# A token-mixing kernel on Trainium2: the entry of the three rounds of chunks is spread differently over the steps

## The chip, the cores and the metric

The kernel runs on one core of a Trainium2 chip. Its time is the device time of one execution in microseconds (us); several runs give a median. The engines are named as in the profile: PE (TensorE, matrix products), DVE (VectorE), ACT (ScalarE), POOL (GpSimd) and SP (SyncE, which here only issues transfers). Transfers between the HBM and the on-chip buffers run on 16 DMA engines; SP, POOL and ACT each have a queue into them and issue in order.

## The reference

First a short causal convolution along the sequence with softmax weights for each of 8 heads, then a phase-aware mixing of tokens and channels. B = 8, S = 4224, D = 192:

```python
out = np.einsum('hk,bskhg->bshg', w, x_unf)         # 7 taps for each of 8 heads
theta = x @ w_theta                                 # x is that result
zr, zi = x * np.cos(theta), x * np.sin(theta)
y = np.einsum('ts,bsd->btd', w_tok_r, zr) + np.einsum('ts,bsd->btd', w_tok_i, zi)
u = x + y
return u + np.maximum(u @ w_ch, 0.0)
```

Nearly all the work is in the two products with 4224 x 4224 matrices, over 8 x 192 = 1536 columns.

## The kernel before

**Tiles.** The sequence is cut into 33 *chunks* of 128 tokens for the inner (source) side and into 33 row blocks of 128 tokens for the output side. A chunk takes 4 pieces of 32 tokens from 4 places of the sequence, so that the weight matrix can be turned in 32 x 32 blocks on DVE. Of each chunk seven half-width tiles are kept in on-chip memory (`z`, one *slot* of 11): the raw products of x with cosine and sine, and sums of them. The two matrices are applied two row blocks (a *unit*) at a time by a scheme with seven multiplications in place of eight, as in Strassen's, whose weight sums (`S1` to `S4`, `wsum`) and z sums (`T1` to `T4`, `sums`) are made on DVE.

**Rounds and steps.** Only 11 chunks are held at a time, so the work goes in three *rounds* of 11 chunks, each of which has to meet all 17 units (16 pairs and one single row block). A *step* t handles one unit `u = (t + shift) % 17` with all chunks that are active at that step: chunk k is active from `start[k]` for 17 steps. `start` comes from the list `base`: chunks enter one or two at a step. In a round's change the old chunks leave and the new ones enter a little later, and n, the number of active chunks, is below 11. There are 58 steps. A step of a pair goes through seven *runs* (`runs`) of n *products* each; a product is two matmuls of 384 columns (L536). At the end of each run of a pair a bank of PSUM is *given* (`give`): DVE adds 128 x 768 values to the sums in `pv` (L461). In the first round some gives are copies on ACT. Three names c1, c2, c3 share two PSUM buffers:

```python
("11", Z11, "c1", True, (0, 0, True)),   ("S1", T1, "c2", True, (1, 1, True)),
("S2", T2, "c1", False, (0, 1, True)),   ("S4", Z22, "c2", False, (0, 1, False)),
("S3", T3, "c1", False, (1, 1, False)),  ("12", Z21, "c3", True, (0, 0, False)),
("22", T4, "c1", False, (1, 0, True)),
```

So c1 is added to in run 7 after the give of run 5 has read it, and c3 in run 6 needs the buffer of c2, which the give of run 4 reads.

**What lies around the products.** The steps' products are one stream (`stream`, `mix`); other work is put into it by hand. `step_events(t)` gives each task a place in sevenths of the step, and the task is emitted before the first product past that place. PE, DVE and ACT keep the order of emission (`in_order`); transfers on SP and chunk loads on POOL may be moved by the scheduler. For a step these are:
- the weights: `load_w` of step t + 2 on POOL (4 DMAs for each matrix; the buffer `st` is free when the turn of the step before has read it), and the turns (L387) and sums (L399) of step t + 1 on DVE (`w_tasks`);
- the sums: `load_rows` brings `pv` of step t + 1 from HBM (`part`), and at a step's end `pv` is stored there; in the last 17 steps it goes on to the output instead. `pv` and the chunks' x tiles `xw` share six buffers (tag `big`);
- the adding of x to the sums: `load_x` and `add_x` (POOL), or for late steps `add_ahead`, two accumulating DMAs on POOL for a row block;
- the chunks: x is loaded (`load_chunk`, 4 DMAs on POOL, and 4 copies on SP of the 16 tokens before each piece out of the chunk before), then built by `tasks`: two convolutions on PE (L216) and their evacuation on ACT, a transpose (L170, ACT), for each half of the columns a theta product on PE (L146) and two sines on ACT (L291), two products with x on DVE (L297), four sums on DVE (L306). `places` gives their places in the step before the chunk enters; with two chunks in a step there are two rows of places.

**The first round** is built ahead of the stream, in a loop over chunks (L812 to L861): between the build's tasks, `between(n)` emits up to n products of the steps whose chunks are ready, 11 at most in one turn of the loop. The `pv` tiles of steps 0 and 1 lie in slots of `z` that later chunks take.

Of the kernel before, what the change touches and what calls it, by code (L numbers as in the profile page):

```python
# [11 lines left out]
F16 = mybir.dt.float16  # L12
# [4 lines left out]
def kernel(  # L17
# [44 lines left out]
    PC = 512  # L62
    NP = 4

    base = [0, 0, 1, 1, 2, 3, 3, 4, 4, 5, 5]
    assert len(base) == NW
    start = [base[k % NW] + (NU + 1) * (k // NW) for k in range(NK)]
    NSTEP = start[-1] + NU
    shift = (NU - 1 - (NSTEP - 1)) % NU

# [109 lines left out]
    Z11, T1, Z21, Z22, T2, T4, T3 = range(7)  # L180
    Z12 = T3

    class Chunk:


# [22 lines left out]
        def conv(self, j):  # L208

            if j == 0:  # L210
                self.z = zpool.tile([P, 7, HN], F16, name="z", tag="z")
                self.x = self.z[:, T2 : T2 + 2, :].rearrange("p t n -> p (t n)")
            pc = banks("pc")
            for h in range(4):
                for half in range(2):
                    pe(nc.tensor.matmul(  # L216
                        pc[half * 2 * Q : (half + 1) * 2 * Q, h // 2,
                           h % 2 * B * G : (h % 2 + 1) * B * G],
                        lhsT=bands[:, 4 * j + h, :, :].rearrange("p a m -> p (a m)"),
                        rhs=self.xw[:, half, :, (4 * j + h) * G : (4 * j + h + 1) * G],  # L220
                        start=True, stop=True,
                    ))
            evacuate(
                self.x.rearrange("p (b d) -> p b d", d=D)[
                    :, :, 4 * j * G : 4 * (j + 1) * G
                ].rearrange("p b (i h g) -> p i h b g", i=2, h=2),
                pc[:, :, 0 : 2 * B * G].rearrange("p i (h b g) -> p i h b g", h=2, b=B),
                self.k == 1 or (self.k in (2, 3) and j == 1),
            )
            if j == 1:  # L230
                self.store()

        def conv_batches(self, g):

            if g == 0:
                self.z = zpool.tile([P, 7, HN], F16, name="z", tag="z")
# [97 lines left out]
    class Step:  # L334


        def __init__(self, t):
# [185 lines left out]
        def mix(self, events):  # L523
# [120 lines left out]
    def step_events(t):  # L644
# [15 lines left out]
        if t in (NPS, NPS + 1):  # L660
            for j, k in enumerate(k for k in range(NK) if start[k] <= NPS):
                for o, a, b, at in (
# [4 lines left out]
                        (1.3 + 1.4 * j if t == NPS else 1.2 + 0.6 * j) + at,  # L667
                        lambda k=k, o=o, a=a, b=b: chunks[k].sum(o, a, b),
                    ))
        if t == NU - 2:  # L670
            def load_wch():
                dve(nc.vector.memset(wch[:, 1:3, :], 0.0))
# [5 lines left out]
            if 0 <= begin < steps[t].time:  # L678
                found.append((7 * begin / steps[t].time, f))
        if t >= NU - 2:  # L680
            new = [k for k in range(NK) if start[k] == t + 2 and k >= NW]
            for k in new:
                found.append((4.5, lambda k=k: load_chunk(k)))
            places = (
                (.1, .1, 1.1, 2.75, 3.05, 3.6, 3.65, 3.9, 4.1),
                (2.1, 2.1, 3.55, 4.6, 5.0, 5.5, 5.55, 5.8, 6.0),
            )
            new = [k for k in range(NK) if start[k] == t + 1 and k >= NW]
            for k, pos in zip(new, places):

                def add(at, j, k):
# [16 lines left out]
    noise = zpool.tile([P, BH], F16, name="noise", tag="z")  # L708
# [76 lines left out]
    flow = stream()  # L785
    need = [None]

    def more(n):

        for i in range(n):  # L790
            if need[0] is None:
                need[0] = next(flow, NK)
            if need[0] > ready[0]:
                return n - i
            need[0] = next(flow, NK)
        return 0

    steps[0].load_rows()
# [4 lines left out]
    for m in (1, 2):  # L803
        steps[1].load_w(m)
    load_chunk(4)
    load_chunk(5)
    for g in range(NG):
        chunks[0].conv_batches(g)
    idle(2)
# [2 lines left out]
    for i in range(1, NW + 2):  # L812
        ch = chunks.get(i) if i < NW else None
        old = chunks[i - 1] if i <= NW else None

        def between(n):
            left = more(n)
            if i < 3:
                idle(min(left, 2) if i == 1 else 0)

        if ch:
            ch.conv(0)
        between(2)
# [6 lines left out]
        between(2)  # L830
# [7 lines left out]
        between(1)  # L838
        if i == 1:
            for first in (Z11, Z21):  # L840
                old.product(first, slice(0, 1))
# [4 lines left out]
                old.product(first, slice(1, 2))  # L846
        elif old:
            old.product(Z11)
        between(2)
# [5 lines left out]
        between(1)  # L855
        if old and start[i - 1] > NPS:
            old.sums(0)
        between(1)
        if old and start[i - 1] > NPS:
            old.sums(1)  # L860
        between(1)  # L861
    ready[0] = NK
    for _ in flow:
        pass
# [31 lines left out]
```

## Time and profile before

| | |
|---|---|
| median of 3 runs | 1435.88 us (1433.75 to 1436.91) |
| the profiled execution | 1437.8 us, span 1436.0 us, mean granted clock 0.999 |
| PE busy | 1409.4 us, 98% |
| DVE busy | 973.0 us, 68% |
| ACT, POOL busy | 310.6 us and 434.3 us |
| DMA | 281.99 MB, 196 GB/s on the mean |

The profile is one execution taken by the hardware profiler. Instructions are grouped by line, engine, operation and tile, with the number, the busy time, the mean of one and the idle time before them with what ended it. A busy PE is not PE at its peak, since matmuls are pipelined and their ends are modelled. The DMA share is the mean busy share of the 16 engines; it can pass 1 where packets of several queues overlap.

### The profile page before, as it was taken

Reading aid. Unit: us, or ns where it says so; the run is one execution under the profiler, and the core shown is the slowest. Engines: PE = TensorE matmul, PEld = TensorE weight load, DVE = VectorE, ACT = ScalarE, POOL = GpSimd, SP = SyncE. Lnnn points to the kernel's source line nnn. Section 1 sums busy time; section 2 is a strip of 40 time slices with the busy share of each in tenths; the row PEclk is TensorE's granted clock in tenths of the full one; section 3 lists DMA queues with packets and bytes.
Section 4 is the critical chain, followed back from the end, with each engine's and each line's share of the span. In section 5 each row is a group of like instructions: output and inputs, shape, how many; then the busy total and the mean of one; then the engine's idle time right before and its main releaser. Section 6 shows DMA issues by size and latency. Waiting matters only on the chain.

```text
span 1436.0 us, 23771 instructions
## 1 busy us (share of the span) xinstructions
PE 1409.4 (98%) x9829; PEld 889.7 (62%) x9829; DVE 973.0 (68%) x1046; ACT 310.6 (22%) x374; POOL 434.3 (30%) x655
## 2 busy tenths in 40 slices
PE   8889999999999999999999999999999999999997
PEld 5556666666666666666666666666566666666665
DVE  6893554545548787866665657877777677767676
ACT  5851101111124244000000004335100110010133
POOL 8511211111233332532333343233323123213110
PEclk9999999999999999999999999999999999999999
DMA  9975766564799999898899889999999999999894
GB/s 193 234 164 132 147 125 128 100 151 89 147 232 227 231 236 239 209 256 177 232 236 229 229 157 243 231 198 255 248 206 216 215 206 220 203 202 197 166 214 136
DMA packets 272045, 281.99 MB, mean 196 GB/s; under 512 B 106688, under 2 KB 240192, under 8 KB 271936
## 3 DMA queue, kind: packets, MB, share of 16 engines
q0 software_dynamic: 162464, 92.15, 48.8%
q1 hardware_dynamic: 71840, 178.88, 35.4%
q10 hardware_dynamic: 37632, 9.44, 4.5%
q8 instruction: 77, 1.26, 0.4%
q14 instruction: 32, 0.26, 0.1%
HBM read 245.49 MB, written 108.13 MB: 246 GB/s over the span
## 4 chain that ended last, share of the span: by engine, by line
PE 92%; DMA 2%; DVE 2%; ACT 1%; SPq 1%; issue 1%; POOL 0%; DVEq 0%; ACTq 0%; POOLq 0%
PE y L536 84%; PE v L146 5%; PE tp L170 1%; PE pc L216 1%; ACT z L291 1%; DMA xw<-in_x_dram 1%; DMA xw<-xw 1%; SPq L194 1%; DVE pv L461 0%; DVE z L306 0%; DVE pv L585 0%; DMA part<-pv 0%; DMA st<-in_moe_w_tok_r_dram 0%; DMA wsb<-in_weight_dram 0%; DVE wt L399 0%
## 5 line engine op out<-in xcount | busy, mean ns | idle before, releaser
L536 PE MATMUL y<-z,wt 128*128 128x384 f16 x7672 | 1282.4, 326 | 6.4 <-DVE pv L461 5.3
L536 PEld LDWEIGHTS <-wt 128*128 128x128 f16 x7672 | 743.7, 98 | 482.6 <-issue 6.3
L461 DVE TENSOR_TENSOR pv<-y,pv 128x768 f32<-128x768 f32 x317 | 302.5, 954 | 323.9 <-PE y L536 284.0
L387 DVE STREAM_TRANSPOSE wt<-st 128x1408 f16<-128x1408 f16 (+7 forms) x224 | 327.5, 1465 | 51.0 <-PE y L536 38.3
L374 POOL DMA_DIRECT2D st<-in_moe_w_tok_r_dram x232 | 132.3, 578 | 463.5 <-DVE wt L387 451.8
L374 POOL DMA_DIRECT2D st<-in_moe_w_tok_i_dram x232 | 132.4, 579 | 405.0 <-DVE wt L387 396.5
L399 DVE TENSOR_TENSOR wt<-wt 128x1408 f16<-128x1408 f16 (+6 forms) x208 | 173.4, 834 | 40.5 <-PE y L536 38.3
L156 ACT ACTIVATE z<-pc 128x768 f16<-128x768 f32 (+1 forms) x62 | 47.5, 803 | 387.0 <-PE pc L216 378.4
L156 ACT ACTIVATE ub<-pv 128x768 f16<-128x768 f32 x63 | 50.2, 836 | 343.6 <-DVE pv L461 315.9
L459 ACT ACTIVATE pv<-y 128x768 f32<-128x768 f32 x66 | 53.7, 814 | 280.5 <-PE y L536 280.5
L146 PEld LDWEIGHTS <-uT 128*128 128x128 f16 x1056 | 90.6, 98 | 23.8 <-issue 5.9
L439 POOL TENSOR_TENSOR pv<-pv,xr 128x1536 f32<-128x1536 f32 x24 | 74.5, 3103 | 66.2 <-issue 26.7
L203 POOL DMA_DIRECT2D xw<-in_x_dram x132 | 76.3, 587 | 27.1 <-issue 7.0
L585 DVE SCALAR_TENSOR_TENSOR pv<-v,pv 128x768 f32<-128x768 f32 (+1 forms) x67 | 62.8, 942 | 24.9 <-PE v L146 24.5
L306 DVE TENSOR_TENSOR z<-z 128x768 f16<-128x768 f16 x132 | 71.2, 552 | 2.2
L291 ACT ACTIVATE z<-v,half_pi 128x768 f16<-128x768 f32 x66 | 59.6, 903 | 56.4 <-PE v L146 55.7
L156 ACT ACTIVATE uT<-tp 128x1536 f16<-128x1536 f16 (+1 forms) x47 | 56.5, 1208 | 47.3 <-PE tp L170 47.3
L297 DVE TENSOR_TENSOR z<-z 128x1536 f16<-128x1536 f16 (+1 forms) x68 | 60.6, 926 | 4.3 <-ACT z L291 4.2
L146 PE MATMUL v<-wth,uT 128*128 128x192 f16 x528 | 54.4, 246 | 2.7 <-ACT z L291 2.1
L146 PE MATMUL v<-wch,uT 128*128 128x192 f16 x528 | 54.3, 246 | 1.3 <-DVE pv L585 0.7
L291 ACT ACTIVATE z<-v 128x768 f16<-128x768 f32 x66 | 53.2, 806 | 0.0
L216 PE MATMUL pc<-xw,bands 96*64 96x192 f16 x512 | 30.4, 251 | 5.4 <-DMA st<-in_moe_w_tok_r_dram 2.7
(45 smaller groups left out, 144.8 us busy)
## 6 DMA issues: line engine op xcount, KB each, us to landing
part<-pv SPq DMA_DIRECT2D x79, 768.0 KB, 4.3
pv<-part SPq DMA_DIRECT2D x79, 768.0 KB, 6.0
out_dram<-pv SPq DMA_DIRECT2D x65, 384.0 KB, 4.5
st<-in_moe_w_tok_r_dram POOLq DMA_DIRECT2D x136, 176.0 KB, 6.0
st<-in_moe_w_tok_i_dram POOLq DMA_DIRECT2D x136, 176.0 KB, 5.3
xs<-z SPq DMA_DIRECT2D x132, 96.0 KB, 5.1
xw<-in_x_dram POOLq DMA_DIRECT2D x121, 96.0 KB, 6.2
xr<-xs SPq DMA_DIRECT2D x24, 384.0 KB, 4.5
```

The costliest lines, as they stand in the source:

```text
L146: pe(nc.tensor.matmul(v[:, k, b * D : (b + 1) * D], lhsT=tT[:, 3 * k + b + i, :], rhs=w[:, 2 * b + i, :], start=(i == 0), stop=(i == 1),))
L156: act(nc.scalar.activation(out=out, in_=in_, func=AT.Copy))
L203: nc.gpsimd.dma_start(out=self.xw[lo : lo + n, h, :, :], in_=x[:, t0 : t0 + n, :].rearrange("b s d -> s b d"),)
L291: act(nc.scalar.activation(**args))
L306: dve(nc.vector.tensor_tensor(out=z[:, o, :], in0=z[:, a, :], in1=z[:, b, :], op=ALU.subtract))
L374: pool(nc.gpsimd.dma_start(out=st[a * Q : (a + 1) * Q, 0:nb, :, 0:n] .rearrange("i r bt s -> i (r bt) s"), in_=w[self.tbs[0] * P : (self.t ...
L387: dve(nc.vector.transpose(self.w[name][:, 0 : self.n, :, :], self.st[int(name[1])][:, int(name[0]) - 1, :, 0 : self.n * Q] .rearrange("p b ...
L399: dve(nc.vector.tensor_tensor(out=self.w[name][:, 0 : self.n, :, :], in0=self.w[a][:, 0 : self.n, :, :], in1=self.w[b][:, 0 : self.n, :, : ...
L439: ins = pool(nc.gpsimd.tensor_tensor(out=self.pv[i], in0=self.pv[i], in1=self.xr[i], op=ALU.add))
L461: dve(nc.vector.tensor_tensor(out=o, in0=yv, in1=o, op=ALU.add))
L536: pe(nc.tensor.matmul(y[cn][:, q, 0:BH], lhsT=self.w[wn][:, c, :, :].rearrange("p bt i -> p (bt i)"), rhs=chunks[k].z[:, zn, q * BH : (q + ...
L585: dve(nc.vector.scalar_tensor_tensor(out=ub[:, ks, :], in0=v[:, ks, :], scalar=0.0, in1=ub[:, ks, :], op0=ALU.max, op1=ALU.add,))
```

## The change

There are now three lists of entries. In the first and second round one chunk enters at a step (after the first four, which enter in pairs), over eight steps instead of five; in the third round entries run from step 39 to 44. The number of steps becomes 61. A new list `build` says in which step a chunk is built: in the first two rounds, as before, the step ahead of its entry; in the third round from step 35 on, mostly one chunk a step, up to four steps ahead of the entry. Chunk loads go into the step ahead of the build as before, but at 1.25 sevenths of it instead of 4.5.

In the loop of the first round `between(n, upto)` no longer emits a fixed number: `reach` counts the products that chunks up to a given one allow, and the products that the newest usable chunk has opened are spread over the whole turn of the loop. Chunk loads in the loop come one turn later.

The `z` slots are taken once ahead of all work (`slots`), and `pv` of steps 0 and 1 and the noise tile lie in named slots. The stores of the sums of steps 0 and 1 (`keep`) are emitted in steps 3 to 6. The window in which x is added early (`quiet`) begins four steps sooner relative to the second round's last entry, and the last nine steps instead of five have x added ahead by accumulating DMAs, one step's row blocks in each of steps 27 and on, the others in step 44.

```diff
-    base = [0, 0, 1, 1, 2, 3, 3, 4, 4, 5, 5]
-    assert len(base) == NW
-    start = [base[k % NW] + (NU + 1) * (k // NW) for k in range(NK)]
+    bases = ([0, 0, 1, 1, 2, 3, 4, 5, 6, 7, 8],
+             [0, 0, 1, 1, 2, 3, 4, 5, 6, 7, 8],
+             [3, 3, 4, 4, 5, 6, 6, 7, 7, 8, 8])
+    start = [b + (NU + 1) * r for r, base in enumerate(bases) for b in base]
+    build = [s - 1 for s in start]
+    build[2 * NW :] = [
+        2 * (NU + 1) + b for b in (-1, -1, 0, 1, 2, 3, 4, 5, 6, 6, 7)
+    ]
...
+    slots = [ztile() for _ in range(NW)]
...
-                self.z = zpool.tile([P, 7, HN], F16, name="z", tag="z")
+                self.z = slots[self.k] if self.k < NW else ztile()
...
-            quiet = [v for v in visits if start[2 * NW - 1] < v <= 2 * NU]
+            quiet = [v for v in visits if start[2 * NW - 1] - 4 < v <= 2 * NU]
+            ahead = t >= NSTEP - 9
...
-                if not self.late:
+                if not ahead:
                     self.adds.append(i)
                 else:
                     far = known <= start[2 * NW - 1]
-                    self.ahead.append((i, 2 * NU - NW + 2 * (t % NU) if far else start[-1],
+                    self.ahead.append((i, start[2 * NW - 1] + t - NSTEP + 10 if far else start[-1],
...
-                    pv = zpool.tile([P, N], F32, name="pv", tag="z")
+                    z = slots[NW - 1 - 2 * self.t - len(self.pv)]
+                    pv = z.rearrange("p t n -> p (t n)")[:, 0 : 2 * N].bitcast(F32)
...
-            if not self.final:
-                for i, tb in enumerate(self.tbs):
-                    nc.sync.dma_start(
-                        out=part[(self.t // NU) % 2][tb, :, :], in_=self.pv[i]
-                    )
+            if not self.final and self.t > 1:
+                for i in range(len(self.tbs)):
+                    self.keep(i)
+
+        def keep(self, i):
+            nc.sync.dma_start(
+                out=part[(self.t // NU) % 2][self.tbs[i], :, :], in_=self.pv[i]
+            )
...
+        if 2 < t < 7:
+            found.append((1, lambda: steps[(6 - t) // 2].keep((6 - t) % 2)))
...
-            new = [k for k in range(NK) if start[k] == t + 2 and k >= NW]
-            for k in new:
-                found.append((4.5, lambda k=k: load_chunk(k)))
+            for k in range(NW, NK):
+                if build[k] == t + 1:
+                    found.append((1.25, lambda k=k: load_chunk(k)))
...
-            new = [k for k in range(NK) if start[k] == t + 1 and k >= NW]
+            new = [k for k in range(NW, NK) if build[k] == t]
...
+    def reach(r):
+
+        return next((i for i, k in enumerate(chunk_of) if k > r), len(chunk_of))
...
-        def between(n):
-            left = more(n)
-            if i < 3:
-                idle(min(left, 2) if i == 1 else 0)
+        lo, hi = reach(i - 3), reach(i - 2)
+
+        def between(n, upto):
+            left = more(max(0, round(lo + (hi - lo) * upto / 13) - done[0]))
+            if i == 1:
+                idle(min(n, 2))
...
-        between(2)
+        between(2, 0)
...
-        if i + 3 < NW:
-            load_chunk(i + 3)
-        between(1)
+        if i > 2:
+            load_chunk(min(i + 2, NW - 1))
+        between(1, 4.5)
...
```

More of the change, by code (lines that the diff above doesn't have):

```diff
@@ L63 @@
     NP = 4
-    base = [0, 0, 1, 1, 2, 3, 3, 4, 4, 5, 5]
-    assert len(base) == NW
-    start = [base[k % NW] + (NU + 1) * (k // NW) for k in range(NK)]
+    bases = ([0, 0, 1, 1, 2, 3, 4, 5, 6, 7, 8],
[6 more added lines that the diff above has]
+    ]
+    assert len(start) == NK and all(
+        start[k] + NU <= build[k + NW] < start[k + NW] for k in range(NK - NW)
+    )
     NSTEP = start[-1] + NU
@@ L181, with ztile @@
     Z12 = T3
+    def ztile():
+        return zpool.tile([P, 7, HN], F16, name="z", tag="z")
+    slots = [ztile() for _ in range(NW)]
     class Chunk:
@@ L235, in conv_batches @@
             if g == 0:
-                self.z = zpool.tile([P, 7, HN], F16, name="z", tag="z")
+                self.z = slots[self.k] if self.k < NW else ztile()
                 self.x = self.z[:, T2 : T2 + 2, :].rearrange("p t n -> p (t n)")
@@ L546, in mix @@
                 f()
-            if not self.final:
-                for i, tb in enumerate(self.tbs):
-                    nc.sync.dma_start(
-                        out=part[(self.t // NU) % 2][tb, :, :], in_=self.pv[i]
-                    )
+            if not self.final and self.t > 1:
[4 more added lines that the diff above has]
+                out=part[(self.t // NU) % 2][self.tbs[i], :, :], in_=self.pv[i]
+            )
         def cast_half(self, i, h, gs, by_dve):
@@ L707 @@
         nc.sync.dma_start(out=stage[i // 2][rows, i % 2, :], in_=part_w)
-    noise = zpool.tile([P, BH], F16, name="noise", tag="z")
+    noise = slots[NW - 5][:, 0, 0:BH]
     nc.vector.memset(noise, 0.0)
@@ L786 @@
     need = [None]
+    done = [0]
+    chunk_of = [s.ks[item[3]] for s in steps for item in s.products()]
+    def reach(r):
+        return next((i for i, k in enumerate(chunk_of) if k > r), len(chunk_of))
     def more(n):
@@ L795, in more @@
             need[0] = next(flow, NK)
+            done[0] += 1
         return 0
@@ L805 @@
     load_chunk(4)
-    load_chunk(5)
     for g in range(NG):
@@ L826 @@
         ready[0] = i - 2
-        between(1)
+        between(1, 1)
         if ch:
             ch.conv(1)
-        between(2)
+        between(2, 3)
         if old:
@@ L835 @@
                 steps[i // 2].turn(name)
-        if i + 3 < NW:
-            load_chunk(i + 3)
-        between(1)
+        if i > 2:
+            load_chunk(min(i + 2, NW - 1))
+        between(1, 4.5)
         if i == 1:
@@ L848 @@
             old.product(Z11)
-        between(2)
+        between(2, 6.5)
         if i > 1 and old:
@@ L854 @@
                 steps[i // 2].turn(name)
-        between(1)
+        between(1, 8)
         if old and start[i - 1] > NPS:
             old.sums(0)
-        between(1)
+        between(1, 9.5)
         if old and start[i - 1] > NPS:
             old.sums(1)
-        between(1)
+        between(1, 11)
     ready[0] = NK
```

## The prediction, written before the result was known

> **What bounds the kernel now.** I read the busy times first, then a table of stretches, then the waits of TensorE, then one step instruction by instruction.
>
> ```profile
> PE 1409.4 (98%) x9829; PEld 889.7 (62%) x9829; DVE 973.0 (68%) x1046; ACT 310.6 (22%) x374; POOL 434.3 (30%) x655
> L461 DVE TENSOR_TENSOR pv<-y,pv 128x768 f32<-128x768 f32 x317 | 302.5, 954 | 323.9 <-PE y L536 284.0
> ```
> TensorE (PE) is busy for 98%, so only the few places where it is not are worth anything. The stretches (columns: busy us of PE, weight load, DVE, ACT, POOL; clock; DMA share; GB/s) find them:
> ```profile
> 20.90:105.20 84.30, 74.13 (x662) 48.39 (x661) 71.73 (x105) 62.77 (x78) 36.51 (x64) 1.00 1.07 207
> 105.20:410.00 304.80, 304.80 (x1878) 183.54 (x1876) 153.32 (x135) 40.51 (x50) 66.08 (x116) 1.00 0.65 133
> 415.30:572.00 156.70, 156.70 (x1255) 103.31 (x1254) 121.16 (x148) 68.58 (x78) 47.63 (x84) 1.00 1.00 233
> 861.60:992.40 130.80, 130.80 (x1042) 86.01 (x1040) 101.27 (x123) 55.46 (x63) 43.19 (x76) 1.00 1.00 224
> 992.40:1038.40 46.00, 42.97 (x316) 27.10 (x314) 35.98 (x39) 13.57 (x16) 16.01 (x24) 1.00 1.04 267
> 1060.00:1340.00 280.00, 280.00 (x1887) 179.33 (x1886) 198.38 (x193) 31.53 (x40) 76.87 (x91) 1.00 0.97 207
> ```
> PE never idles in either change of rounds up to 992 us, nor in the long stretches: nothing can be gained there, only lost. Idle are the entry of the first round (20.9 to 105.2) and 3.0 us in steps 40 and 41. Counting the L536 pairs against the steps' sizes, a product (two matmuls) takes 0.325 us. A chunk's build takes PE 0.79 (convolutions) + 0.67 (transposes) + 2 x 0.66 (thetas) + some 0.17 at the seams = 2.95 us. The entry holds 132 products, 42.9 us, and 398 other matmuls, 9.05 chunks at 44 each, 26.7 us: 69.6 of 84.3, so **14.7 us are lost there**, most of it inside "busy".
>
> The waits of PE name what it falls behind when it idles:
> ```profile
> PE y L536 <- DVE pv L461: 5.3, 5, 1.9
> PE pc L216 <- DMA st<-in_moe_w_tok_r_dram: 2.7, 2, 2.3
> PE pc L216 <- DMA xw<-xw: 2.7, 2, 2.0
> ```
> And this is how close DVE stands in step 39 (966.2 to 992.4; nine active chunks, two being built). First ACT's sines of the first chunk, then DVE, then PE:
> ```profile
> 977.64 0.90 ACT L291 ACTIVATE z<-v,half_pi 128x768 f16<-128x768 f32 x1 [1.53 <-PE v L146]
> 978.44 0.80 ACT L291 ACTIVATE z<-v 128x768 f16<-128x768 f32 x1
> 979.28 0.90 ACT L291 ACTIVATE z<-v,half_pi 128x768 f16<-128x768 f32 x1
> ```
> ```profile
> 980.21 1.83 DVE L297 TENSOR_TENSOR z<-z 128x1536 f16<-128x1536 f16 x2 [0.96 <-ACT z L291]
> 982.55 0.96 DVE L461 TENSOR_TENSOR pv<-y,pv 128x768 f32<-128x768 f32 x1 [0.51 <-PE y L536]
> 983.42 2.20 DVE L306 TENSOR_TENSOR z<-z 128x768 f16<-128x768 f16 x4
> 985.54 1.37 DVE L387 STREAM_TRANSPOSE wt<-st 128x1152 f16<-128x1152 f16 x1
> 986.84 0.92 DVE L461 TENSOR_TENSOR pv<-y,pv 128x768 f32<-128x768 f32 x1
> ```
> ```profile
> 976.78 0.82 PE L146 MATMUL v<-wth,uT 128*128 128x192 f16 x8
> 986.59 6.01 PE L536 MATMUL y<-z,wt 128*128 128x384 f16 x36
> ```
> Run 7 adds to the bank that the fifth give (986.84 to 987.76) reads. Run 6 began at 986.59 and has nine products, so run 7 begins at 989.52: the fifth give was ready 1.8 us before it was needed. That chain (theta, sines, two products, give, four sums, turn, give) is fixed in length; PE's way to run 7 shrinks with the number n of active chunks. The change makes n small exactly while third-round chunks are built.
>
> **The change, part by part.** Work on PE is equal (19660 instruction rows in both programs, the same tables of products); steps go from 58 to 61. The sum is against the profiled execution, 1437.8 us (span 1436.0, 1.8 around it), which lies 1.9 over the median of the three runs, 1435.88.
>
> *Third round: built at steps 35 to 43, entered at 39 to 44.* Between, n is 9, 7, 6, 5, 6, 7, 7, 8, 9 in steps 35 to 43 (before: 9 or 10 in 35 to 40). The order of DVE in the built program is that shown above in each of them. In a step with one build, the first theta follows item 14, 17 or 20 for n = 5, 6, 7; so it starts at n=5 14 x 0.325 + 0.79 + 0.67 + 0.17 = 6.2 us after the step begins, at n=6 7.15, at n=7 8.1. From it to the end of the third sine are 3.40 us (976.78 to 980.18), and then 0.03 + products 1.74 + give 0.87 + sums 2.12 + turn + give 0.92. The turn is for the next step's n', less 0.07 of overlap; these rows exist:
> ```profile
> L387 DVE STREAM_TRANSPOSE wt<-st 128x896 f16<-128x896 f16 x8 | 8.8, 1102 | 0.0
> L387 DVE STREAM_TRANSPOSE wt<-st 128x768 f16<-128x768 f16 x4 | 3.9, 969 | 0.0
> L387 DVE STREAM_TRANSPOSE wt<-st 128x640 f16<-128x640 f16 x4 | 3.4, 842 | 7.0 <-DMA st<-in_moe_w_tok_r_dram 5.0 <-PE y L536 2.1
> ```
> Run 7 could begin at 6n x 0.325 + 2.95 us. Step 38 (n=5, n'=6): give ready at 6.2 + 3.4 + 5.65 + 0.9 = 16.15, run 7 at 12.7: 3.45 lost. Step 37 (6, 5): 17.0 against 14.65, 2.35. Step 39 (6, 7): 2.65. Step 36 (7, 6): 18.1 against 16.6, 1.5. Step 40 (7, 7): 1.65. Step 41 (7, 8; its turn between the rows of 896 and 1152 columns, 1.2): 1.8. **Sum +13.4 us**. The same sum for n=10 with one build leaves 1.2 us to spare, so the second round's entry (n=10, steps 19 to 25) costs 0; if a row is half a microsecond worse it still costs nothing, and it cannot gain. Ends for the third: 0, if all of it were hidden as in 861 to 992, and +25, if transfers come late too (below). I take +13.4, since every term is a row of the neighbouring step.
>
> *Steps 43 and 44 for 40 and 41.* One build instead of two stands in the short step: DVE has 1.83 + 2.2 us less, PE 2.95 less. Before, 3.0 us idle there, partly a turn that waited 3.1 us for its weights. The last give of the short step's first bank comes some 2 us late now, and weights may again: 2 to 5 us, against 3.0. I take no difference, ends -2 and +3.
>
> *First round, a chunk a step, products spread over each build.* In the slot after chunk 1's convolution there is nothing, then 4, 20, 4, 24, 36, 43, 50, 57, 64, 71 products (before: 4, then 9 and 11 each). From the sixth on PE has 14.6 us or more of its own in each build, and ACT (two evacuations, four sines, one turn: 1.51 + 3.40 + 1.45 = 6.4, and gives at 0.81) no longer sets the pace. What stays lost: slots of four products, PE 4.25 against ACT 6.4, about 1.2 in the one and 2.2 in the other; chunk 5's load, which now stands on POOL behind the weights of step 2 (issued at 30.8 to 33.2 before), so it is issued by 35.5, lands in 6.2 (median of xw loads) at 41.7, where it is wanted at about 41: 1 to 2; DVE, which in slots 5 and 6 has about 10.6 and 14.9 us of turns, sums, products and gives against PE's 10.7 and 14.6 and starts 3 behind, because it waits for step 2's weights as it did before (5.0 us): 3. With 1 for later slots that is 9 of the 14.7: **-5.7 us**. Ends: -12, if only the slots of four stay, and +2, if the longer ramp waits for weights at each step.
>
> *First sums stored late.* The four stores of steps 0 and 1 (768 KB, 6.8 us to land in this stretch) are written later in the program, but in the built order of SP one still stands ahead of chunk 5's copies of history, one behind them. They free no buffer that PE waits for; their row blocks are read 17 steps later. Before, two stores held up SP to 31.5 and 38.7 us, and chunk 5's convolution idled 2.0 for xw<-xw. This is inside the -5.7; alone its ends are -2 and +1.
>
> *Chunk loads a step ahead.* On POOL they now stand between a step's two weight loads, 4 issues of 0.58 = 2.3 us ahead of the second, which waits for the turn at 4.2 sevenths of its step anyway. In 861 to 992 they landed in 8.0 us at the median with no PE idle. 0, ends 0 and +3 (if the second load comes those 2.3 late).
>
> *Additions and traffic.* Adds of x on POOL go from 24 to 19 (3.1 each, never on the path), adding DMAs from 18 to 28, 14 of them in step 44 where 8 stood in step 41. PE had no idle from 1024 on with eight in flight; 0, ends 0 and +4. Six more stores and six more loads of sums lie in full steps or in the narrow ones.
>
> Total +13.4 - 5.7 = +7.7: 1445.5 as that execution counts, **1444 us as a median**.
>
> **The rivals.** *The entry wins (faster).* If DVE's chain were covered, the entry alone would decide: 3 in the middle and -9 at the front give 1430. For it: DVE was 101.3 of 130.8 us busy in 861 to 992, and with one build a step instead of two its load per build interval falls. Against it: the chain is of latencies in one step, not of load. It decides once steps 36 to 41 lose under 5.7 together. The Trainium skill's page Perfetto Trace Analysis, section Optimization Strategy, says that where the most contended engine changes over time, interleaving the regimes may help; by that rule spreading both entries gains, and the time is this rival's. In the entry the rows agree with it, in steps 36 to 41 I think not.
>
> *The DMA engines bind in the narrow steps (slower still).* Each step moves four 768 KB blocks whatever its n, 128 packets of 6 KB at 234 ns each: 7.5 us of 16 engines; weights for n=7 are 2048 packets at 55 ns, 7.0 us; chunk load, history and store 5. That is 19.5 us in step 38, against 17.8 with DVE's loss. For it: share 1.00 already in 861 to 992. Against: 20.9 to 105.2 ran at 1.07. It would add 2 to 3 us in four steps: 1453. The packet records show 704 bytes in 74 ns, 448 in 55, 320 in 46: smooth. The Trainium skill's DMA: Bandwidth & Descriptors, section Specifications, puts line rate at 512 bytes and more, with read-modify-write below; at twice the price for n of 7 and less the steps would need some 26 us, an estimate that gives about 1480. The records do not bear that out.
>
> *The entry gains nothing.* The ramp waits for weights instead: 1449. For it: two waits for st in the list above.
>
> **How the numbers follow.** The forecast 0.60 (1439 to 1449 by its terms), entry wins 0.18, DMA binds 0.12 (0.02 of it for 1480), no gain in the entry 0.10. About 0.2% (2.9 us) is what a measurement here can tell from no change. Faster by more takes most of the second case, 0.16; within it 0.07, from the edges of the first two; slower 0.77. The range 1431 to 1454 reaches from the faster case's time to just past the DMA case.
>
> **What would show it.** Right: steps 36 to 41 last 17 to 18 us with PE waiting for the give (L461's successor) just before run 7, most in step 38; PE loses 8 to 10 us rather than 14.7 up to the first step that runs at full rate. Wrong: no PE wait for DVE near 770 to 890 us, or waits there that end with a transfer; an entry that loses 15 again, with PE waiting for xw or DVE for st.

## The result and the profile after

The changed kernel takes **1461.39 us** (1460.85 to 1461.98 in four runs), the kernel before 1435.87 beside it: a ratio of 1.018, with a 95% interval of 1.0162 to 1.0197. Slower was right, but 25.5 us instead of the 8 forecast, and the time lies above the range of 1431 to 1454. The profiled execution of after has a span of 1459.1 us, 23.1 more than that of before; the other 2.4 are no part of the two traces, since the profiled execution of before lay 1.9 over its median and that of after 0.5 under.

The first fence shows lines of the page of after, the second its table of stretches (columns as before: busy us of PE, weight load, DVE, ACT and POOL; clock; DMA share; GB/s), the third the waits of PE over the whole span.

```profile
PE 1412.2 (97%) x9829; PEld 889.9 (61%) x9829; DVE 995.9 (68%) x1091; ACT 310.5 (21%) x374; POOL 442.7 (30%) x684
L476 DVE TENSOR_TENSOR pv<-y,pv 128x768 f32<-128x768 f32 x338 | 322.2, 953 | 315.7 <-PE y L551 275.1
```
```profile
20.80:100.00 79.20, 72.04 (x599) 45.86 (x597) 59.75 (x87) 50.95 (x64) 38.83 (x68) 1.00 1.16 222
534.00:593.00 59.00, 55.02 (x391) 34.45 (x389) 46.74 (x47) 13.17 (x16) 23.21 (x26) 1.00 0.92 220
850.00:1070.00 220.00, 200.06 (x1491) 127.64 (x1490) 172.43 (x212) 67.26 (x78) 76.38 (x128) 1.00 1.06 252
1080.00:1360.00 280.00, 280.00 (x1887) 179.34 (x1886) 199.41 (x194) 31.53 (x40) 69.90 (x91) 1.00 0.94 201
```
```profile
PE y L551 <- DVE pv L476: 23.1, 19, 2.1
PE v L154 <- DMA uT<-ub: 6.8, 1, 6.8
```

PE's busy time is nearly the same; what grew is its idle time: in the second round's entry (534 to 593 us), where it had none before, in the third round's (850 to 1070), where it had 3.0 us, and in one long wait for a transfer after that. A step begins with its first L551 product, so each step's length can be read from the trace and compared with its products at 0.325 us and 2.95 us for each chunk built. (Steps with a build that lose nothing come out 0.07 us short for each chunk, so a build really takes 2.88; differences that small count as nothing below.) For before and after this gives (us):

| where | before | after | difference |
|---|---|---|---|
| first round, time up to the first step at full rate (4 before, 8 after) less the products ahead of it | 62.3 | 58.3 | -4.1 |
| steps 22 and 23 (10 chunks, one built) | none lost | 27.91 and 27.78 long, their neighbours 25.63 | +4.4 |
| step 28 | 0 | 0.7 | +0.7 |
| third round, steps 36 to 41 | 0 (36, 37, 39) | 1.34, 2.18, 3.94, 3.49, 2.84, 1.76 | +15.55 |
| last steps of that entry (38, 40, 41 before; 43, 44 after) | 3.7 | 1.7 | -2.1 |
| step 45 | as its neighbours | 36.22 long, its neighbours 27.66 | +8.6 |

The sum is +23.1, the difference of the spans. Two of the rows, +4.4 and +8.6, are not in the prediction at all.

### The profile page after: what moved, and what is told of

The parts are those of the page before. It is cut to its first block, busy times and chain, and to the rows that moved or that the text cites. A ratio compares the mean times of both kernels' runs of the same rounds, so it can differ in the third digit from the quotient of the medians.

```text
span 1459.1 us, 23864 instructions
## 1 busy us (share of the span) xinstructions
PE 1412.2 (97%) x9829; PEld 889.9 (61%) x9829; DVE 995.9 (68%) x1091; ACT 310.5 (21%) x374; POOL 442.7 (30%) x684
## 4 chain that ended last, share of the span: by engine, by line
PE 81%; DMA 8%; DVE 7%; issue 1%; POOL 1%; ACT 1%; SPq 0%; DVEq 0%; POOLq 0%; ACTq 0%
PE y L551 73%; PE v L154 5%; DVE pv L476 2%; DVE wt L401 2%; DVE z L310 1%; PE tp L178 1%; DMA uT<-ub 1%; PE pc L229 1%; DVE z L319 1%; DMA xs<-z 1%; DMA xw<-xw 1%; DMA st<-in_moe_w_tok_i_dram 1%; DMA part<-pv 1%; DMA xr<-xs 1%; DVE wt L413 1%
## 5 line engine op out<-in xcount | busy, mean ns | idle before, releaser
L551 PE MATMUL y<-z,wt 128*128 128x384 f16 x7672 | 1285.9, 326 | 25.8 <-DVE pv L476 23.1
L551 PEld LDWEIGHTS <-wt 128*128 128x128 f16 x7672 | 743.5, 98 | 506.4 <-issue 24.9
L476 DVE TENSOR_TENSOR pv<-y,pv 128x768 f32<-128x768 f32 x338 | 322.2, 953 | 315.7 <-PE y L551 275.1
L401 DVE STREAM_TRANSPOSE wt<-st 128x1408 f16<-128x1408 f16 (+8 forms) x236 | 328.8, 1398 | 43.2 <-PE y L551 35.9
L388 POOL DMA_DIRECT2D st<-in_moe_w_tok_i_dram x244 | 139.6, 580 | 449.5 <-DVE wt L401 428.8
L388 POOL DMA_DIRECT2D st<-in_moe_w_tok_r_dram x244 | 139.5, 579 | 420.9 <-DVE wt L401 410.3
L413 DVE TENSOR_TENSOR wt<-wt 128x1408 f16<-128x1408 f16 (+7 forms) x220 | 173.0, 786 | 47.2 <-PE y L551 45.0
L474 ACT ACTIVATE pv<-y 128x768 f32<-128x768 f32 x58 | 47.1, 812 | 211.1 <-PE y L551 210.4
L454 POOL TENSOR_TENSOR pv<-pv,xr 128x1536 f32<-128x1536 f32 x19 | 59.9, 3152 | 58.5 <-DVE pv L603 16.4
L319 DVE TENSOR_TENSOR z<-z 128x768 f16<-128x768 f16 x132 | 74.4, 574 | 2.2
L310 DVE TENSOR_TENSOR z<-z 128x1536 f16<-128x1536 f16 (+1 forms) x68 | 63.6, 967 | 5.1 <-ACT z L304 5.0
```

The source lines that it names most:

```text
L310: dve(nc.vector.tensor_tensor(out=o, in0=xv, in1=o, op=ALU.mult))
L319: dve(nc.vector.tensor_tensor(out=z[:, o, :], in0=z[:, a, :], in1=z[:, b, :], op=ALU.subtract))
L388: pool(nc.gpsimd.dma_start(out=st[a * Q : (a + 1) * Q, 0:nb, :, 0:n] .rearrange("i r bt s -> i (r bt) s"), in_=w[self.tbs[0] * P : (self.t ...
L401: dve(nc.vector.transpose(self.w[name][:, 0 : self.n, :, :], self.st[int(name[1])][:, int(name[0]) - 1, :, 0 : self.n * Q] .rearrange("p b ...
L413: dve(nc.vector.tensor_tensor(out=self.w[name][:, 0 : self.n, :, :], in0=self.w[a][:, 0 : self.n, :, :], in1=self.w[b][:, 0 : self.n, :, : ...
L476: dve(nc.vector.tensor_tensor(out=o, in0=yv, in1=o, op=ALU.add))
```

## The experiments

Each run is one kernel; where no interval is given it is one timed execution, on a chip where before took 1435.4 us (experiments 1, 2, 4 and the first run of 6), 1437.1 (3, 5, the second run of 6, the first of 9) or 1436.6 (7, 8, the second run of 9). Differences in single steps are read from its trace.

**1. The burst of adding transfers in step 44.**

```diff
-    self.ahead.append((i, start[2 * NW - 1] + t - NSTEP + 10 if far else start[-1],
+    self.ahead.append((i, start[2 * NW - 1] + t - NSTEP + 10 if far else start[-1] + t - NSTEP + 9,
```

> The changed kernel, with the adding DMAs that all stood in step 44 spread over steps 44 to 52, one step's row blocks each. Theory (the burst holds up the transposing DMAs of step 44, for whose result PE waits in step 45): step 45 takes 27.7 us instead of 36.2, the transposes land in under 11 us instead of 20, and the time falls by 8 to 9 us. Rival (the adding DMAs cost the same wherever they stand): the loss of 8.6 us is found again spread over steps 45 to 53, and the time stays within 2 us.

Measured: 1451.93 us, 9.5 less than after; step 45 is 27.66 long. What happens in after, first the instructions on ACT and its queue, then those on PE, then the transfers issued from 1028 to 1090 us (KB each, median us from issue to landing):

```profile
1052.68 1.43 ACTq L171 DMA_TRANSPOSE uT<-ub  x1
1054.65 1.58 ACT L164 ACTIVATE ub<-pv 128x768 f16<-128x768 f32 x2 [2.00 <-DVE pv L476]
1056.26 14.91 ACTq L171 DMA_TRANSPOSE uT<-ub  x1
```
```profile
1059.79 6.18 PE L551 MATMUL y<-z,wt 128*128 128x384 f16 x37
1072.80 1.46 PE L154 MATMUL v<-wch,uT 128*128 128x192 f16 x8 [6.83 <-DMA uT<-ub]
```
```profile
part<-xs POOLq DMA_DIRECT2D x14, 384.0 KB, 10.1
...
uT<-ub ACTq DMA_TRANSPOSE x3, 20.1
```

Step 45 is the first in the kernel that applies the channel matrix to finished sums. They are transposed by DMA from ACT's queue, and PE wants the result at once. The 14 accumulating transfers of 384 KB were issued from 1038.96 to 1058.37, the last five of them behind the first transpose. That transpose, issued at 1052.68, landed only after 20 us, and the second sat 14.9 us in ACT's queue; PE, which takes its work in order, stood 6.8 us for it. The median landing of all 24 transposes is 6.6 us. Most of the other 1.7 of the 8.6 us came right after the wait: from 1072.8 to 1076 the profile shows TensorE's granted clock at 0.50, and its matmuls of 384 columns came 0.32 us apart in place of 0.163. With the transfers spread over steps 44 to 52 (they go out in five of these steps, one or two row blocks at a time), the longest landing is 11.2 us and PE waits for no transpose. So the cause is that the transfers stand together beside the transposes, not how many the kernel has: there are 28 in both. Whether the transposes lost to the transfers in the DMA engines or in the order in which these take up queues is not told apart.

**2. The additions of x on POOL, moved within their step.** Step 22 of after has two additions on POOL (L454), step 23 has one. The second, from 546.45 to 549.56, ran beside a give and a turn and held up neither. Here are the other two in the order of time, with start and length in us, each with what runs beside it on DVE, and the wait of PE behind the last:

```profile
534.72 4.72 DVE L310 TENSOR_TENSOR z<-z 128x1536 f16<-128x1536 f16 x2
...
534.94 3.69 POOL L454 TENSOR_TENSOR pv<-pv,xr 128x1536 f32<-128x1536 f32 x1 [5.00 <-DVE wt L413]
...
564.37 3.92 DVE L319 TENSOR_TENSOR z<-z 128x768 f16<-128x768 f16 x2
564.46 3.42 POOL L454 TENSOR_TENSOR pv<-pv,xr 128x1536 f32<-128x1536 f32 x1 [6.51 <-DVE z L310]
...
569.21 0.97 PE L551 MATMUL y<-z,wt 128*128 128x384 f16 x5 [1.92 <-DVE pv L476]
```

A pair of products of x (L310) takes 1.8 us elsewhere, here 4.72; a pair of z sums (L319) takes 1.14, here 3.92. The gives behind them come late, and PE waits 2.05 us for one in step 22 and 1.92 in step 23. The spread of all instructions of these lines (ns, min/median/max) shows it too:

```profile
L310 DVE TENSOR_TENSOR z<-z x68: 516/951/3857, 17.6 to 1022.9; 128x1536 f16<-128x1536 f16 x64, 128x768 f16<-128x768 f16 x4
...
L319 DVE TENSOR_TENSOR z<-z x132: 514/552/3333, 38.7 to 1025.4; 128x768 f16<-128x768 f16 x132
```

```diff
-    found.append((3.6 + 2 * i, lambda i=i: steps[t + 1].add_x(i)))
+    found.append((4.3 + 1.3 * i, lambda i=i: steps[t + 1].add_x(i)))
```

> The changed kernel, with the adds of x on POOL put later in their step (4.3 and 5.6 sevenths instead of 3.6 and 5.6), behind the chunk's products and sums. Theory (a POOL add and a DVE instruction with two inputs in on-chip memory hold each other up): in steps 22 and 23 no product or sum on DVE takes over 1 us (3.9 and 3.3 now), both steps last 25.6 us instead of 27.9 and 27.8, and the time falls by 4 to 4.5 us. Rival (those steps wait for a transfer, and DVE's long rows are how the wait shows): both steps stay at 27 us or more.

Measured: 1460.6 us, only 0.8 less. Step 22 lost nothing now, step 23 1.23, and step 24 2.45, which had lost nothing: together 3.7 in place of 4.3 by the same count. The additions had met another line of DVE, the weight sums (L413), whose 872 ns at the median became 3152 at the most:

```profile
540.02 0.92 DVE L476 TENSOR_TENSOR pv<-y,pv 128x768 f32<-128x768 f32 x1
540.86 3.15 DVE L413 TENSOR_TENSOR wt<-wt 128x1280 f16<-128x1280 f16 x1
543.93 0.94 DVE L476 TENSOR_TENSOR pv<-y,pv 128x768 f32<-128x768 f32 x1
```

The addition ran from 540.24 to 543.33 beside them. The give at 540.02, which reads one operand from PSUM, kept its 0.92 us; the weight sum, with both operands in on-chip memory, ended 0.7 us after the addition did. The miss of this run therefore speaks for the mechanism, but it did not yet show that the time in steps 22 and 23 is its price.

**3. The additions of steps 22 and 23 taken away.** Their three row blocks get accumulating transfers some steps later instead (34 such transfers in all, 28 in after).

```diff
-    quiet = [v for v in visits if start[2 * NW - 1] - 4 < v <= 2 * NU]
+    quiet = [v for v in visits if start[2 * NW - 1] < v <= 2 * NU]
```

> The window for early additions begins again after the second round's last entry, so the additions of steps 22 and 23 leave POOL there and become adding transfers some ten steps later. Theory (in those steps an addition on POOL and a product or sum on DVE with two operands in on-chip memory hold each other up, 3.3 to 3.9 us for instructions that else take 0.55 and 0.95): steps 22 and 23 return from 27.91 and 27.78 to the 25.63 of their neighbours, 4.4 us less in all, and every L310 and L319 instruction of the second round takes 0.51 to 0.96 us. Rival (the two steps are late for another reason, the loads of the chunk or of the weights): they stay at 27.8 and the time within 1 us of 1461.4.

Measured: steps 22 and 23 are 25.63 us long, 4.4 less in all, and no instruction of the two lines is held:

```profile
L310 DVE TENSOR_TENSOR z<-z x68: 517/951/960, 17.8 to 1019.4; 128x1536 f16<-128x1536 f16 x64, 128x768 f16<-128x768 f16 x4
...
L319 DVE TENSOR_TENSOR z<-z x132: 515/552/561, 38.3 to 1021.9; 128x768 f16<-128x768 f16 x132
```

In the other runs that keep these additions in their places, the two steps lose 4.4 to 6.2 us. The whole kernel took 1458.69, 2.7 less. Step 28 lost nothing here, but that proves nothing: in most of the other runs with the change it loses nothing either. In this execution the entry was 1.7 us longer and the burst's step 1.1 longer than in the profile of after (over the runs that keep the burst that step varies from 36.0 to 38.1).

**4. The sums of third-round chunks moved behind a turn.** In the one-build steps after 35:

```diff
+            if t > 35 and len(new) == 1:
+                places = (places[0][:7] + (5.5, 6.5),)
```

> The changed kernel, with the four sums of a third-round chunk at 5.5 and 6.5 sevenths of its build step instead of 3.9 and 4.1, behind the fifth give; no transfer is moved. Theory (the fifth give comes late by what DVE has ahead of it): the give comes 2.1 us sooner in each of steps 36 to 41; by the same rows as before steps 36 to 41 lose 0, 0.8, 2.2, 1.0, 0.2 and 0.2 us, 4.4 in place of 15.6, so the time falls by 9 to 12 us. Rival (the transfers bind in the narrow steps): the six steps keep their 119.7 us within 2 us, and PE waits end with transfers.

Measured: 1453.1 us, 8.3 less, a little short of the 9 to 12 expected. Steps 36 to 41 lose -0.07, 0.43, 2.59, 1.88, 1.15 and -0.07, 5.9 instead of 15.55; what is left stands in steps 38 to 40, for a reason shown under the third round below. Step 43 no longer loses its 1.7, and step 44 now loses 1.4, because the sums of the last chunk reach into it. First the waits of PE from 860 to 1060 us in after, then the same in this run:

```profile
PE y L551 <- DVE pv L476: 15.9, 11, 2.0
```
```profile
PE y L551 <- DVE pv L476: 6.4, 7, 1.6
```

Nothing was taken off DVE: four sums (2.2 us) only stand behind a turn and a give instead of ahead of them. So most of the loss is the position of the give in a chain of fixed length, as the prediction had it.

**5. The chunks entered sooner, built as before.**

```diff
-             [3, 3, 4, 4, 5, 6, 6, 7, 7, 8, 8])
+             [1, 1, 2, 2, 3, 4, 5, 6, 7, 8, 8])
```

> Third-round chunks are built in the same steps, but enter one to three steps sooner (37, 37, 38, 38, 39, 40, 41, 42, 43, 44, 44), so that 7, 8 and then 9 chunks are active in steps 36 to 43 instead of 7, 6, 5, 6, 7, 7, 8, 9. Theory (the chain of DVE is fixed in length and what it costs is set by n alone): by the sum of the prediction step 36 still loses 1.5, step 37 with n=8 about 0.7, the later ones nothing, 2 to 4 us in place of the 15.5 measured there. The end gets more narrow steps (9, 7, 6, 5, 4, 3, 2 chunks in steps 54 to 60 against 11, 11, 9, 7, 6, 4, 2); by the losses of the present steps 56 to 59 (3.0, 4.2, 4.5, 7.2) that costs some 6 to 7 us. Net -5 to -7. Rival (the loss comes from the builds or their loads, not from the narrowness): steps 36 to 41 keep 10 us or more of their loss, and the time rises to 1463 to 1468.

Measured: 1453.83 us, 7.6 less. Steps 36 to 41 lose 1.70, 0.99, then 0.02 in each, 2.8 in all. The builds and their loads are in the same steps as in after, so it is the number of active chunks that decides. Steps 53 to 59 lose 32.0 us where after loses 26.7, so the longer end costs 5.2. In steps 36 to 43 PE is busy but for 3.9 of 179 us, with DVE's share of the stretch (140.3 of 179) as high as it is in after's (172.4 of 220):

```profile
869.00:1048.00 179.00, 175.07 (x1311) 112.16 (x1310) 140.30 (x165) 55.25 (x63) 50.40 (x90) 1.00 1.02 244
```

**6. The entry of the first round.** Two runs take the two parts of it one by one. The first keeps the new lists and goes back to a fixed number of products in a turn of the loop (in it later chunks overwrite the sums of steps 0 and 1 in their slots ahead of the late stores, so it serves for its time alone; the work is the same):

```diff
-    left = more(max(0, round(lo + (hi - lo) * upto / 13) - done[0]))
+    left = more(n)
```

> The changed kernel, with the loop of the first round emitting at most 11 products a turn again, with the new lists of entries kept. Theory (the gain of the entry comes from giving PE enough products in each build): the full rate is reached with the loss of before, so the time rises by 3 to 6 us. Rival (the gain comes from the lists alone, or from the stores that were moved): the time stays within 1.5 us.

The second has the lists, windows, additions and stores of before, with the new loop and the early chunk loads:

```diff
-    bases = ([0, 0, 1, 1, 2, 3, 4, 5, 6, 7, 8],
-             [0, 0, 1, 1, 2, 3, 4, 5, 6, 7, 8],
-             [3, 3, 4, 4, 5, 6, 6, 7, 7, 8, 8])
+    bases = 3 * ([0, 0, 1, 1, 2, 3, 3, 4, 4, 5, 5],)
...
```

> The three lists of before (and its windows, additions and stores), with the changed kernel's loop of the first round: the products that a chunk opens are spread over the next chunk's build, chunks are loaded a turn later, and later chunks are loaded at 1.25 sevenths of a step. Theory (spreading the products is worth 2 to 3 us by itself, as the run with the old pacing and the new lists showed in the entry): 1432 to 1434, the gain wholly before step 4. Rival (with two chunks a step the pieces are too uneven, and the later loads cost what the spreading gains): 1435 to 1438.

Measured: 1462.41 and 1441.61 us. The entries, counted as in the table of the result (for the second run up to step 6, since its builds reach into step 5):

| lists, loop | us |
|---|---|
| old, old (before; the run of experiment 8, whose entry is the same) | 62.3; 63.6 |
| new, old | 60.3 |
| old, new | 68.5 |
| new, new (after, and eight other runs) | 58.3 (57.4 to 59.9) |

One and the same entry varies by 1.3 to 2.5 us from one execution to the next, so these are rough sizes. Neither part is worth 4 us by itself: the lists are worth 2 to 3 alone, the spreading of products another 1.7 on top of them (on the mean of the nine, 58.6), and with the old lists it costs 5 to 6. The time of the first run, 1.0 above that of after, is its rival's; its entry is 2.0 longer. Theory and rival of the second run both fell. In that run PE waits from 20 to 157 us mostly for ACT and DVE (the three longest are shown), where the two longest in before are for transfers:

```profile
PE v L149 <- ACT z L299: 3.9, 4, 1.2
PE y L546 <- DVE z L305: 2.5, 1, 2.5
PE y L546 <- DVE pv L471: 2.5, 2, 2.0
```

Why pairs of entries and a spread stream go so badly together was not tried further.

**7. First sums stored late.** The changed kernel with those stores at the end of steps 0 and 1 again:

```diff
-            if not self.final and self.t > 1:
+            if not self.final:
...
-        if 2 < t < 7:
-            found.append((1, lambda: steps[(6 - t) // 2].keep((6 - t) % 2)))
```

> The changed kernel with the four stores of the first sums at the end of steps 0 and 1, as before. Theory (they free nothing that TensorE waits for): the time stays within 1.5 us of 1461.4, and step 8 starts between 175 and 178 us as in the other runs with this entry. Rival (the late stores are what made room on SP for the loads, and part of the entry's 4 us is theirs): step 8 starts at 178 to 180 us and the waits for xw grow by 1 to 2 us.

Measured: 1460.7 us, step 8 starts at 176.57 (after: 176.24), and every step up to there has the length that it has in after within 0.01 us. The place of these stores is worth nothing.

**8. Chunk loads a step ahead, alone on the kernel before.**

```diff
-                found.append((4.5, lambda k=k: load_chunk(k)))
+                found.append((1.25, lambda k=k: load_chunk(k)))
```

> The kernel before with one part of the change alone: chunk loads at 1.25 sevenths of their step in place of 4.5. The run with the old lists and the new pacing lost 2.0 us less than before in step 41 and 0.3 in step 38, where a turn of before waited for its weights. Theory (the early load leaves POOL free for the second load of weights, and that is the gain): 1432.5 to 1434.5, ratio 0.998 to 0.999. Rival (the profiled execution of before lay 1.9 over its median by just that wait, which most executions do not have): 1435 to 1437, ratio 0.9995 to 1.001.

Measured over 12 runs: 1436.4 us against 1436.58, ratio 0.9999 (0.999 to 1.0008). Its trace has 1.7 us less in step 41 and 0.3 less in step 38 than that of before, but the interval excludes a gain of 2 us. That is the rival's time, and it would follow if the wait of step 41 in the profile of before is not in its usual execution. With one trace of before this is not shown; in the trace of this run an entry 1.3 us longer than that of before hides most of the gain.

**9. The repairs together, and a list in between.** The edits of 1, 3 and 4:

> Three repairs at once: the adding transfers of step 44 spread over steps 44 to 52, the early window for additions as before, and the sums of third-round chunks after step 35 moved behind the step's turn (5.5 and 6.5 sevenths). Theory (the three losses are separate and add up): -9.4, -4.4 and -8.3 from 1461.4 give 1439 (1437 to 1441), step 45 at 27.7 and steps 22 and 23 at 25.6. Rival (they cover each other, so that one repair uncovers another loss): 1443 or more.

Measured: 1439.55 us. Step 45 is 27.66, steps 22 and 23 are 25.63, and steps 36 to 41 lose 5.9 us: the losses are separate and add up. (Step 44 keeps the loss that the moved sums brought, 1.7 here.) Then, with the same edits, the third list `[2, 2, 3, 3, 4, 5, 6, 6, 7, 8, 8]`:

> The three repairs of the earlier run, with third-round entries between the two lists tried so far (38, 38, 39, 39, 40, 41, 42, 42, 43, 44, 44) and the builds where the change put them, so that 7, 6, 7, 8, 8, 8, 9, 9 chunks are active in steps 36 to 43. Theory (narrowness against the length of the end): steps 36 to 41 lose about 0.6 instead of 6.0, the end about 2.5 us more, 1436 to 1438, the same as before within 0.2%. Rival (an addition uncovers another loss, as spreading the entry did): 1440 or more.

Measured over 11 runs: 1436.3 us against 1436.58 of before, ratio 0.9998 (0.9989 to 1.0008). In steps 36 to 44 only step 37 still loses (1.88), steps 55 to 59 lose 24.2 instead of 21.5 there. No kernel tried is faster than before by more than can be measured.

## Why the prediction was wrong in size

The forecast failed at its term "Additions and traffic": it was put at 0 with 4 us as its upper end, and it measured 13. Every other term missed by 2.2 us or less; that the third round's miss (+2.2) and that of steps 43 and 44 (-2.1) cancel is luck.

**The entry of the first round** (-5.7 predicted, -4.1 in the profile, -3.7 on the mean of nine runs with this entry, or -4.4 for the mean against the other trace with the old entry). Direction right. Counted in the prediction's way, 10.7 us are still lost there where it forecast 9. PE's waits up to step 8 are 6.9 of them: 3.4 for DVE (3 forecast), 2.8 for ACT (1.2 and 2.2), 0.7 for xw (1 to 2 for chunk 5's load). The other 3.8 lie inside PE's busy time, and against them the prediction has only 1 us "for later slots"; so far as the waits tell, that is the term that was too small, and why it was stays open. The prediction also did not see that the lists and the spreading have to come together.

**First sums stored late, and chunk loads a step ahead** (0 each): right, experiments 7 and 8.

**The third round** (+13.4 predicted, +15.55). The mechanism was right: PE waits just ahead of run 7 in each narrow step, for the give that it named, and for the give ahead of run 6 too. Its additions are off by no more than 0.1 us in a term. The terms of steps 36, 37 and 41 were 1.5, 2.35 and 1.8 and measured 1.34, 2.18 and 1.76. Those of 38 to 40 were 3.45, 2.65 and 1.65 and measured 3.94, 3.49 and 2.84. The step that failed there is "0.03 + products": a weight sum of the next step stands ahead of the products on DVE and waits for TensorE. In step 39 of after, on DVE:

```profile
934.88 0.61 DVE L413 TENSOR_TENSOR wt<-wt 128x896 f16<-128x896 f16 x1
936.61 0.63 DVE L413 TENSOR_TENSOR wt<-wt 128x896 f16<-128x896 f16 x1 [1.12 <-PE y L551]
937.15 1.82 DVE L310 TENSOR_TENSOR z<-z 128x1536 f16<-128x1536 f16 x2
938.89 0.95 DVE L476 TENSOR_TENSOR pv<-y,pv 128x768 f32<-128x768 f32 x1
939.76 2.20 DVE L319 TENSOR_TENSOR z<-z 128x768 f16<-128x768 f16 x4
941.88 1.10 DVE L401 STREAM_TRANSPOSE wt<-st 128x896 f16<-128x896 f16 x1
942.91 0.92 DVE L476 TENSOR_TENSOR pv<-y,pv 128x768 f32<-128x768 f32 x1
```

The reader sees the predicted chain line by line, and ahead of it a weight sum that starts 0.2 us after PE begins run 5 (936.41). The third sine ended at 936.07, so the products start 1.1 us late; run 7 follows the last give at 943.88. The same wait stands ahead of the products in step 38 (0.7 us from the third sine to the first product) and in step 40 (1.4); in steps 36, 37 and 41, where the terms fit, the gap is 0.03, 0.03 and 0.13.

**Steps 43 and 44** (0, with ends of -2 and +3): -2.1, at the lower end. Against the usual execution of before, which by experiment 8 may lack the wait in step 41, the true term lies nearer 0.

**The second round's entry** ("costs 0 ... it cannot gain"): the chain of waits there does fit, and steps 19 to 21, 24 and 25 lost nothing. The 4.4 us came from the other engine, out of the next term.

**Additions and traffic** (0, ends 0 and +4) is where the prediction failed; it measured +13, 4.4 in steps 22 and 23 and 8.6 in step 45. Two of its steps do not hold. First the lines of before that bear on them:

```profile
L399 DVE TENSOR_TENSOR wt<-wt x208: 415/881/3016, 43.9 to 1401.1; 128x1408 f16<-128x1408 f16 x68, 128x1152 f16<-128x1152 f16 x22, 128x896 f16<-128x896 f16 x4, 128x1280 f16<-128x1280 f16 x4
...
L163 ACTq DMA_TRANSPOSE uT<-ub x24: 1292/1936/6420, 1037.7 to 1345.6; - x24
...
DMA to landing us min/median/max: 4.9/7.3/10.9
```

- "Adds of x on POOL ... never on the path". POOL's own end is not on the path, but an addition there keeps DVE from its work. The row that would have told it was in the trace of before: the weight sums there took 415/881/3016 ns (least, median, most), and the one of 3016 lay beside an addition from 604.48 to 607.58. The change moved three additions from full steps, where DVE has time to spare, into steps with a build, where the instruction that is held is a link of DVE's chain.
- "PE had no idle ... with eight in flight". Eight transfers had been free, so fourteen were priced at nothing. But the last of the eight was issued at 1037.40, ahead of the first transpose at 1037.7; five of the fourteen came behind it. The transposes that share the DMA engines with them were not looked at, though in before they had already landed in 7.3 us at the median and 10.9 at the most, and PE takes their result next.

**The rivals.** "The entry wins" needed less than 5.7 us in steps 36 to 41; they lost 15.55. The spreading that it rests on gained 4 us in the entry and lost there. "The entry gains nothing" fell with those 4 us. "The DMA engines bind" fell as well: the DMA share was 1.06 from 850 to 1070, but every wait of PE there names DVE, and experiments 4 and 5 removed most of them while the share stayed at 1.0 or above (1.16 from 890 to 990 in the run of experiment 4). The Trainium skill's page DMA: Bandwidth & Descriptors, section Specifications, has packets under 512 bytes below line rate. The estimate of 1480 us that went with it is not borne out, since TensorE waited for no transfer in those steps.

## What to carry to other kernels

Spreading a pipeline's refill over more steps makes each step narrower, and a chain of fixed latency that was hidden in a wide step then sets its length; price the chain against the narrowest step, with every instruction that stands ahead of it in its engine's queue. Read the largest duration of a group, not only its mean: one instruction three times longer than its median, beside an instruction of another engine, can be the mark of a shared resource, and a change that moves either of them moves the hit. When transfers are gathered in one step, look at which other transfers are issued there and who waits for them at once.

## What the hardware showed that was not expected

An addition on POOL with both operands in on-chip memory (3.10 us alone) and a DVE instruction of the same kind do not run beside each other at all. The product that began at 535.59, 0.65 us after the addition, took 3.86 us and ended 0.8 after the addition's end, nearly its own 0.95 later; the addition in its turn took 3.69, 0.6 longer than alone, and for its first 0.7 an earlier product still ran. Gives (one operand in PSUM, 0.95) and turns (one operand, 1.64 at full width) kept their times beside additions in every run. The Trainium skill's page SBUF — State Buffer, section Who interferes with whom, says so: a VectorE instruction with two inputs in SBUF and a GpSimd instruction that reads SBUF exclude each other, and whichever came first has the shared path for its whole length. The trace agrees, with the numbers above.

A second thing was the size of the hit that a burst of accumulating transfers gives to DMA transposes: 6.6 us to land at the median, 20.9 at the most beside fourteen transfers of 384 KB, and 14.9 us in which ACT's queue could issue nothing else.
